# Up products of a bilinear layer: 15 products for three channel tiles and two token halves, with five additions of each triple on GpSimd

## The chip, the core and the metric

The kernel runs on one core of one Trainium2 chip. Its time is the device time of one execution in microseconds (us); the median of several runs is compared. TensorE is called PE in the profile (PEld for its weight loads), VectorE is DVE, ScalarE is ACT, GpSimd is POOL, and SyncE, which issues nearly all transfers here, is SP.

## What is computed

A linear attention with a decaying state (4 batches, 8 heads, 768 tokens, 48 channels a head), followed by a bilinear layer on the 3072 tokens with their 384 channels (1536 inner channels). All is fp32.

```python
for t in range(S):
    state = f[:, :, t, :, None] * state + np.einsum('bhd,bhe->bhde', k[:, :, t], v[:, :, t])
    y[:, :, t] = np.einsum('bhd,bhde->bhe', q[:, :, t], state)
...
a = x @ w_a
b = x @ w_b
return (a * b @ w_out).astype(np.float32)
```

## The kernel before

The 3072 tokens are eight blocks of 384 (BLK), two to a batch. For each block the attention has two units of four heads; their result lands transposed in xT (channels on the partitions: 3 tiles of 128 by 384 tokens). The up products a and b of a block are 12 inner tiles of 128 channels (NFT) by 384 tokens each, contracted over 3 channel tiles. Their elementwise product goes to a part of `groups`, and down products bring it back to 384 channels.

*Blocks 1 and 2* (the first batch) are made by up (L463): for one inner tile, 3 matmuls of 384 tokens for b and 3 for a, into two of the four PSUM banks ps_f; product (L478) copies b to SBUF on ScalarE (L484) and multiplies on VectorE (L486).

*Blocks 3 to 8* are made by up_pair (L528), two inner tiles (j) at a time, for both a and b (g). Of the three channel tiles, the first two are handled as a 2x2x2 block product (two inner tiles, two channel tiles, two token halves of 192) with 7 products for 8; the third takes 4. That is 11 calls of times (L540), each of two matmuls (b and a) of 192 tokens (L542). The products are accumulated in the four banks in such an order that intermediate sums are copied out once by ScalarE (L550, L553, L555, L559) and added to by VectorE (four additions L547 of a PSUM bank and an SBUF tile, called at L560 to L568); the two multiplications a*b per pair are L572. up_pair yields twice a pair, 12 times a block. The operands other than plain tiles are sums: of w, made once by combine_w_ba (L500; 8 VectorE instructions of 768 elements, L514) into the four `raw` buffers that the weight conversion has left; and of x, made for each block by combine_x (L520; four VectorE instructions of 192 elements, L526).

*Down* (L593) takes two groups of 128 tokens and makes 7 products for 8 in the same manner (L610), of 6 matmuls each. VectorE forms the sums s3, s1, s2, s4 in three rotating tiles `h` of 768 elements (L605 through the helper add), ScalarE copies u2, u3 and c11, VectorE adds, and SP stores the result tile o (L645, L649). Its first sum s3 is issued ahead of the last up products of the block; x1 needs s2, which needs the second half of the block's products.

*Attention*, for one unit u: front (L254) computes two sigmoids on ScalarE (L262 with an accumulator read, L264), one instruction on GpSimd (L266, 768 elements), two scans (L271), six scans (L281) and the products with q and k (L283, L284) on VectorE; then scores (matmuls L319, masked by L335), turn (transposes L347, copy to kT L351), gains (L367, sums L383), within (L401), across (L422, three copies y L435 and transfers to xT L450). front for the next unit is spread over the yields of slot (L652).

*Order of the work.* The program is written out by hand; each engine executes its instructions in the order in which they are called. The list `rest` holds the up and down work, and a counter `step` grows by one for each up, by one for each yield of up_pair and by 0.5 for each part of down. After each of these, beside (L844) continues the generators in `queue` that are due at that step: the slots of the attention, and combine_w_ba at 15.6, 16.6, 17.6 and 18.6 (L840). The plain up of blocks 1 and 2 ends with step 23, up of block 3 begins after 34.5. combine_x for the next block is called in the fifth part of the down ahead of it (L883). In the first 125 us the weights, which arrive as doubles, are converted: four ScalarE instructions, one on GpSimd (L205, 1.2 to 2.8 us) and two on VectorE (L214, L216); at the end combine_w_out (L580) makes the sums for down (L588 to L591).

The second kernel, by_levels, stands behind a condition on the data that doesn't hold here; the trace has none of its instructions.

Of the kernel before, what the change touches and what calls it, by code (L numbers as in the profile page):

```python
# [21 lines left out]
BLK = 384  # L22
# [11 lines left out]

# [3 lines left out]
def kernel(  # L44
# [30 lines left out]
    with tc.If(again > 0), ExitStack() as pools:  # L75
        by_levels(pools, tc, q, k, f_logit, v, masks, out, ident, weights)


def by_quotients(ctx, tc, q, k, f_logit, v, moe_w_a, moe_w_b, moe_w_out, out, ident, weights, bad):
# [27 lines left out]

# [18 lines left out]
    invs = [fixed([128, 2 * BLK], "inv"), spare[:, 3 * PIECE + PIECE // 2:3 * PIECE + PIECE // 2 + 2 * BLK]]  # L126
    tails = fixed([128, NU], "tails")
# [33 lines left out]
    def pieces():  # L161

        for ft, n in [(0, 1)] + [(ft, 2) for ft in range(1, NFT - 1, 2)] + [(NFT - 1, 1)]:
            for dst, src in ((w_b, moe_w_b), (w_a, moe_w_a)):
                cols = slice(ft * 128, (ft + n) * 128)
                yield dst[:, :, cols], src.rearrange("(kt p) c -> p kt c", p=128)[:, :, cols], (NKT, n * 128)
        for ft in range(0, NFT, 2):
            rows = moe_w_out[ft * 128:(ft + 2) * 128]
            yield w_out[:, ft:ft + 2], rows.rearrange("(k p) c -> p k c", p=128), (2, DM)

    EARLY = (4, 5)
    todo, raws, going = list(pieces()), [], []
# [18 lines left out]
    def from_double(dst, raw, k, bit):  # L191

        words = raw.bitcast(U32).rearrange("p k (n two) -> p (k n) two", two=2)
        lo, hi = words[:, :, 0], words[:, :, 1]
        width = lo.shape[1]
        h = sb3.tile([128, PIECE], FP32, tag="h", name="h")[:, 0:width]  # L200
        bit, sgn = bit[:, 0:width], sign[:, 0:width]
        nc.scalar.activation(h, hi.bitcast(FP32), AF.Abs, scale=HI_SCALE)  # L202

        nc.scalar.activation(bit.bitcast(FP32), lo, AF.Identity, bias=whole, scale=2.0**-29)
        nc.gpsimd.tensor_scalar(h, h, HI_MAX, None, ALU.min)  # L205
        yield
        nc.scalar.activation(sgn, hi.bitcast(FP32), AF.Sign)

        nc.scalar.activation(
            bit.bitcast(U16).rearrange("p (n two) -> p n two", two=2)[:, :, 1], sgn, AF.Relu, scale=-32768.0  # L210
        )
        yield
        hu = h.bitcast(U32)
        nc.vector.tensor_scalar(hu, hu, 3, None, ALU.logical_shift_left)  # L214
        hu, bit = (x.rearrange("p (k n) -> p k n", k=k) for x in (hu, bit))
        nc.vector.tensor_tensor(dst.bitcast(U32), hu, bit, ALU.add)  # L216
        yield

    def begin(n):

        while 2 * n > begun[0] < 2 * len(todo):
            i, second = divmod(begun[0], 2)
            dst, src, shape = todo[i]
            if not second:
                going.append(from_double(dst, raws[i], shape[0], bits[i % len(bits)]) if src.dtype != FP32 else iter(()))
            next(going[i], None)
            begun[0] += 1
# [65 lines left out]
    turns = itertools.cycle((0, 1))  # L293
# [184 lines left out]
    def product():  # L478
# [4 lines left out]
        b_sb = sb2.tile([128, BLK], FP32, tag="b_sb", name="b_sb")  # L483
# [6 lines left out]


    HT = BLK // 2
    sums_of_w, sums_of_x = [], {}

    def by_pairs(k):

        w = w_ba[:, :, k].rearrange("p g (j two c) -> p g two j c", two=2, c=128)
        return w[:, :, 0], w[:, :, 1]

    def combine_w_ba():  # L500

        (a11, a21), (a12, a22) = by_pairs(0), by_pairs(1)
        for _ in range(4):
            raw = raw_pool.tile([128, PIECE], mybir.dt.uint64, tag="raw", name="raw")
            sums_of_w.append(raw.bitcast(FP32).rearrange("p (g j c) -> p g j c", g=2, c=128))
        s1, s2, s3, s4 = sums_of_w
        for to, x, y, op in (
            (s3, a11, a21, ALU.subtract),
            (s1, a21, a22, ALU.add),
            (s2, s1, a11, ALU.subtract),  # L510
            (s4, a12, s2, ALU.subtract),
        ):
            for g in range(2):
                nc.vector.tensor_tensor(to[:, g], x[:, g], y[:, g], op)  # L514
            yield

    def blocks_of_x(blk, k):
        return (xT[blk][:, k, HT * i:HT * i + HT] for i in range(2))

    def combine_x(blk):  # L520

        (b11, b12), (b21, b22) = blocks_of_x(blk, 0), blocks_of_x(blk, 1)
        tiles = (sb2.tile([128, BLK], FP32, tag="b_sb", name="b_sb") for _ in range(2))
        t1, t2, t3, t4 = sums_of_x[blk] = [t[:, HT * i:HT * i + HT] for t in tiles for i in range(2)]
        for to, x, y in ((t1, b12, b11), (t2, b22, t1), (t3, b22, b12), (t4, b21, t2)):
            nc.vector.tensor_tensor(to, x, y, ALU.subtract)  # L526

    def up_pair(blk, j):  # L528

        (a11, a21), (a12, a22), (a1, a2) = (by_pairs(k) for k in range(NKT))  # L530
        (b11, b12), (b21, b22), (b1, b2) = (blocks_of_x(blk, k) for k in range(NKT))
        s1, s2, s3, s4 = sums_of_w
        t1, t2, t3, t4 = sums_of_x[blk]
# [717 lines left out]
```

## Time and profile before

| | |
|---|---|
| median of 3 runs | 626.2 us (626.1 to 627.07) |
| span of the profiled execution | 624.1 us; no other time of it is given, 2.1 us lie between it and the median |
| mean granted TensorE clock | 0.989 |
| plain up, blocks 1 and 2, to the end | until 145.5 us |
| down of the first batch | 145.5 to 202.4 us |
| up of blocks 3, 4, 5, 6, 7, 8 | 202.4, 267.2, 345.3, 409.8, 487.9 and 547.4 us to 249.6, 314.0, 392.2, 456.7, 533.0 and 590.4 us |
| last down | 590.4 to 624.1 us |
| up matmul records L542 | 1584, 296.6 us busy together |
| additions L547 on VectorE | 144, 557 ns each |
| multiplications L572 on VectorE | 72, 550 ns each |
| copies L550, L553, L555, L559 on ScalarE | 36 each, 479 ns |
| GpSimd after 125 us | L266 alone, 0.83 us each where nothing holds it |

A group's mean duration of a matmul (327 ns for 192 tokens) is longer than its share of PE's time, because matmuls overlap; the distance between the starts of groups says what one costs. In the order of time of one engine a line gives the start, the time until the end of the group, the engine, the line of the kernel, what is written and read, and in brackets the idle time ahead of it and what ended that.

### The profile page before, as it was taken

The numbers are of one execution on the slowest core, as the hardware profiler recorded it, in microseconds if no ns is written. First come the engines' busy times: TensorE is split into PE (matmuls) and PEld (weight loads), VectorE is DVE, ScalarE is ACT, GpSimd is POOL, SyncE is SP. The second block draws the span as 40 slices with busy tenths as digits, with TensorE's granted clock in tenths as the row PEclk, the third lists the DMA queues.
The fourth block names the chain that finished last, engine by engine and source line by source line (L and its number), as shares of the span: only waits on it lengthen the run. The fifth ranks groups of instructions, "written<-read, shape, count | busy, mean of one in ns | idle before, by whom it ended". The sixth has DMA issues, their size and how long they took to land.

```text
span 624.1 us, 13969 instructions
## 1 busy us (share of the span) xinstructions
PE 588.6 (94%) x5922; PEld 534.5 (86%) x5922; DVE 377.8 (61%) x748; ACT 221.6 (36%) x400; POOL 63.0 (10%) x58
## 2 busy tenths in 40 slices
PE   0759899999999999999999999999999999999995
PEld 0626555558998999999999999999999999999995
DVE  6777445797877567746676476756665244534541
ACT  5578499822332243224312332233311232022200
POOL 6334154410000000000000000000000000000000
PEclk9969999999999999999999999999999999999998
DMA  8886875000045404040404003050001000000000
GB/s 215 230 274 188 181 254 193 1 1 1 32 121 114 100 2 96 6 118 1 97 1 120 28 14 85 1 122 2 21 0 46 26 8 13 2 27 0 1 26 30
DMA packets 30343, 43.65 MB, mean 70 GB/s; under 512 B 3776, under 2 KB 24896, under 8 KB 30272
## 3 DMA queue, kind: packets, MB, share of 16 engines
q1 hardware_dynamic: 29984, 42.38, 25.2%
q8 instruction: 48, 0.79, 0.6%
q10 hardware_dynamic: 288, 0.30, 0.2%
q14 instruction: 23, 0.19, 0.1%
HBM read 33.23 MB, written 4.72 MB: 61 GB/s over the span
## 4 chain that ended last, share of the span: by engine, by line
PE 89%; DMA 4%; ACT 2%; DVE 2%; SPq 1%; issue 0%; ACTq 0%; DVEq 0%
PE ps_f L542 42%; PE ps_f L610 25%; PE ps_f L469 14%; DMA xT<-y 2%; PE ps_x L319 2%; PE ps_y L401 2%; PE ps_x L367 2%; PE ps_y L422 1%; PE ps_x L347 1%; DMA raw<-in_moe_w_b_dram 1%; DMA q_in<-in_q_dram 1%; SPq L154 1%; DVE h L605 0%; SPq L150 0%; ACTq L450 0%
## 5 line engine op out<-in xcount | busy, mean ns | idle before, releaser
L542 PE MATMUL ps_f<-xT,w_ba 128*128 128x192 f32 x864 | 155.7, 327 | 0.0
L547 DVE TENSOR_TENSOR groups<-ps_f,groups 128x384 f32<-128x384 f32 x144 | 80.1, 557 | 117.6 <-ACT groups L559 102.5
L542 PEld LDWEIGHTS ps_f<-xT,w_ba 128*128 128x128 f32 x864 | 142.3, 190 | 0.6
L469 PE MATMUL ps_f<-xT,w_ba 128*128 128x384 f32 x288 | 97.3, 497 | 7.5 <-DVE w_ba L216 6.0
L469 PEld LDWEIGHTS ps_f<-xT,w_ba 128*128 128x128 f32 x288 | 54.9, 193 | 47.1 <-DVE w_ba L216 7.1
L542 PE MATMUL ps_f<-b_sb,raw 128*128 128x192 f32 x432 | 82.2, 326 | 0.0
L542 PEld LDWEIGHTS ps_f<-b_sb,raw 128*128 128x128 f32 x432 | 72.2, 190 | 0.2 <-ACT groups L550 0.2
L610 PE MATMUL ps_f<-w_out,h 128*128 128x192 f32 x288 | 51.8, 330 | 0.0
L550 ACT COPY groups<-ps_f 128x384 f32<-128x384 f32 x36 | 17.2, 479 | 94.9 <-PE ps_f L542 94.8
L610 PE MATMUL ps_f<-w_out,groups 128*128 128x192 f32 x288 | 50.9, 327 | 0.0
L610 PE MATMUL ps_f<-spare,h 128*128 128x192 f32 x288 | 49.4, 327 | 0.2 <-DVE h L605 0.2
L610 PEld LDWEIGHTS ps_f<-w_out,groups 128*128 128x128 f32 x288 | 47.4, 190 | 0.1
L610 PEld LDWEIGHTS ps_f<-w_out,h 128*128 128x128 f32 x288 | 46.8, 190 | 0.6
L610 PEld LDWEIGHTS ps_f<-spare,h 128*128 128x128 f32 x288 | 46.8, 190 | 0.7 <-issue 0.5
L205 POOL TENSOR_SCALAR h<-h 128x768 f32<-128x768 f32 (+1 forms) x20 | 40.7, 2035 | 49.9 <-ACT h L202 49.9
L266 POOL TENSOR_SCALAR inv<-inv 128x768 f32<-128x768 f32 x14 | 13.5, 962 | 303.8 <-ACT inv L262 301.6
L572 DVE TENSOR_TENSOR groups<-groups 128x384 f32<-128x384 f32 x72 | 36.6, 550 | 0.0
L605 DVE TENSOR_TENSOR o<-ps_f,u 128x192 f32<-128x192 f32 x36 | 12.9, 357 | 39.1 <-PE ps_f L610 38.9
L559 ACT COPY groups<-ps_f 128x384 f32<-128x384 f32 x36 | 17.2, 479 | 53.0 <-PE ps_f L542 53.0
L435 ACT COPY y<-ps_y 48x384 f32<-48x384 f32 (+1 forms) x43 | 20.5, 476 | 25.9 <-PE ps_y L422 21.5
L542 PE MATMUL ps_f<-xT,raw 128*128 128x192 f32 x144 | 29.4, 327 | 0.0
L542 PE MATMUL ps_f<-b_sb,w_ba 128*128 128x192 f32 x144 | 29.3, 326 | 0.0
(113 smaller groups left out, 691.3 us busy)
## 6 DMA issues: line engine op xcount, KB each, us to landing
q_in<-in_q_dram SPq DMA_DIRECT2D x32, 144.0 KB, 4.5
k_in<-in_k_dram SPq DMA_DIRECT2D x32, 144.0 KB, 3.6
v_in<-in_v_dram SPq DMA_DIRECT2D x16, 288.0 KB, 5.1
raw<-in_moe_w_out_dram SPq DMA_DIRECT2D x6, 768.0 KB, 4.4
out_dram<-o SPq DMA_DIRECT2D x24, 192.0 KB, 1.9
f_in<-in_f_logit_dram SPq DMA_DIRECT2D x28, 144.0 KB, 3.0
xT<-y SPq DMA_DIRECT2D x46, 72.0 KB, 2.2
raw<-in_moe_w_b_dram SPq DMA_DIRECT2D x4, 768.0 KB, 7.3
```

The source lines that it names most:

```text
L205: nc.gpsimd.tensor_scalar(h, h, HI_MAX, None, ALU.min)
L266: nc.gpsimd.tensor_scalar(inv, inv, EXP_K, 1.0, ALU.mult, ALU.add)
L319: nc.tensor.matmul(ps[h][SUB * p:SUB * p + SUB, o:o + SUB], lhsT=kf[r, tokens(n, c, p)], rhs=qf[r, tokens(n, c, p)], start=True, stop=True,)
L435: copy(y[r:r + rows, :, p], ps[p][e:e + rows, 0:BLK].rearrange("r (o m) -> r o m", m=SUB))
L469: nc.tensor.matmul(ps[nm][:, 0:BLK], lhsT=w[:, kt, ft * 128:ft * 128 + 128], rhs=x[:, kt], start=kt == 0, stop=kt == NKT - 1,)
L542: nc.tensor.matmul(to[:, g], lhsT=w[:, g, j], rhs=x, start=start and g == 0, stop=True, skip_group_check=True)
L547: nc.vector.tensor_tensor(c[:, :, k, i], x, y, ALU.add)
L550: nc.scalar.copy(p1, x0)
L559: nc.scalar.copy(u3, x0)
L572: nc.vector.tensor_tensor(to[:, :, 2 * j + k], a[:, :, k], b[:, :, k], ALU.mult)
L605: nc.vector.tensor_tensor(to, x, y, op)
L610: nc.tensor.matmul(to, lhsT=x[:, i], rhs=w[:, i], start=first and i == 0, stop=i == HFT - 1, skip_group_check=True)
```

## The change

Up products of blocks 3 to 8 are made by up_triples in place of up_pair: three inner tiles (j of 4) at a time, all three channel tiles, two token halves, with 15 products for 18, named v1 to v6, u1 to u5, t1, t2, r2, r3 after the bank in which they are summed. In each bank the next product is added to the last after an intermediate state was copied out. Of the results, six are written by a ScalarE copy (`first`, and the one in `finish`), four additions read PSUM on VectorE (`add`), and for five more ScalarE copies the bank to a temporary and GpSimd adds the temporary to the result (`late`). `finish` (v6, its copy and one VectorE multiplication of 1152 elements) of a triple is called behind the first product of the next one, and for the last triple of a block at once. up_triples yields three times a triple, 12 times a block as before.

combine_w_ba makes six sums and two tiles of w_ba in place, in 26 GpSimd instructions of 512 elements, at steps 15.6 to 22.8 (nine times two) and from 24.2 on (four times two). combine_x makes its sums in 11 VectorE instructions, some in place in xT. The tiles h and b_sb lie at fixed places in `sums` and `x_sums`, as many as before (three and two); u3 of down lies in o. In by_levels, which isn't executed, the weights are converted anew.

```diff
@@ -124,6 +174,13 @@
     bits = [spare[:, PIECE * i:PIECE * i + PIECE].bitcast(U32) for i in range(3)]
     sign = spare[:, 3 * PIECE:3 * PIECE + PIECE // 2].bitcast(BF16)
     invs = [fixed([128, 2 * BLK], "inv"), spare[:, 3 * PIECE + PIECE // 2:3 * PIECE + PIECE // 2 + 2 * BLK]]
+
+    sums = fixed([128, 3 * PIECE], "sums")
+    thirds = [sums[:, PIECE * i:PIECE * i + PIECE] for i in range(3)]
+    blocks = itertools.cycle(thirds)
+    last = groups[:, NTG + 1:2 * NTG].rearrange("p g c -> p (g c)")
+    x_sums = fixed([128, 5 * (BLK // 2)], "x_sums")
+    b_copies = itertools.cycle([x_sums[:, BLK * i:BLK * i + BLK] for i in range(2)])
     tails = fixed([128, NU], "tails")
     held = fixed([128, NU, 2], "held")
 
...
@@ -480,102 +501,168 @@
         if not factors:
             return
         blk, ft, ps = factors.pop(0)
-        b_sb = sb2.tile([128, BLK], FP32, tag="b_sb", name="b_sb")
+        b_sb = next(b_copies)
         nc.scalar.copy(b_sb, ps["b"][:, 0:BLK])
         a, b = (x.rearrange("p (g t) -> p g t", g=NTG) for x in (ps["a"][:, 0:BLK], b_sb))
         nc.vector.tensor_tensor(products(blk)[:, :, ft], a, b, ALU.mult)
         give_back(ps.values())
 
 
-
-
     HT = BLK // 2
-    sums_of_w, sums_of_x = [], {}
-
-    def by_pairs(k):
-
-        w = w_ba[:, :, k].rearrange("p g (j two c) -> p g two j c", two=2, c=128)
-        return w[:, :, 0], w[:, :, 1]
...
     def combine_w_ba():
 
...
+        halves = []
         for _ in range(4):
...
+            raw = raw_pool.tile([128, PIECE], mybir.dt.uint64, tag="raw", name="raw").bitcast(FP32)
+            halves += [raw[:, 512 * i:512 * i + 512].rearrange("p (j c) -> p j c", c=128) for i in range(3)]
+        s = [halves[2 * i:2 * i + 2] for i in range(6)]
+        (a11, a12, a13), (a21, a22, a23), (a31, a32, a33) = (
+            [[w_ba[:, g, k].rearrange("p (j i c) -> p i j c", i=NI, c=128)[:, i] for g in range(2)] for k in range(NKT)]
+            for i in range(NI)
+        )
         for to, x, y, op in (
...
+            (s[0], a21, a32, ALU.add),
+            (s[1], a12, a22, ALU.add),
+            (s[2], s[1], a21, ALU.add),
+            (s[1], s[1], a23, ALU.add),
+            (s[3], a12, s[1], ALU.subtract),
+            (s[3], s[3], a32, ALU.subtract),
+            (s[4], a31, a11, ALU.subtract),
+            (s[5], s[4], a32, ALU.add),
+            (s[4], a33, s[4], ALU.subtract),
+            (a22, s[1], s[4], ALU.subtract),
+            (a22, a22, a13, ALU.add),
+            (a31, a31, a33, ALU.subtract),
+            (a31, a31, a21, ALU.add),
         ):
             for g in range(2):
...
+                nc.gpsimd.tensor_tensor(to[g], x[g], y[g], op)
             yield
...
+        sums_of_w.update(
+            v1=s[0], v2=a32, v3=s[3], v4=s[1], v5=a12, v6=s[2],
+            u1=a21, u2=a31, u3=s[4], u4=a11, u5=s[5],
+            t1=a22, t2=a13, r2=a23, r3=a33,
+        )
 
     def combine_x(blk):
 
...
+        x = xT[blk].rearrange("p k (i t) -> p k i t", i=2)
+        (b11, b12), (b21, b22), (b31, b32) = ([x[:, k, i] for i in range(2)] for k in range(NKT))
+        s = x_sums.rearrange("p (n t) -> p n t", t=HT)
+        more = last[:, 2 * NI * BLK:].rearrange("p (n t) -> p n t", t=HT)
+        u5, u3, v6, v1, u1 = (s[:, n] for n in range(5))
+        v2, v4, t2, r2 = (more[:, n] for n in range(4))
+
+        def op(to, x, y, op):
+            nc.vector.tensor_tensor(to, x, y, op)
+
+        op(s[:, 0:2], x[:, 0], b31.unsqueeze(1).broadcast_to((128, 2, HT)), ALU.add)
+        op(v1, b21, u5, ALU.subtract)
+        op(v6, b31, b21, ALU.subtract)
+        op(b11, b11, b12, ALU.subtract)
+        op(u1, b11, v6, ALU.add)
+        op(r2, b22, b32, ALU.subtract)
+        op(v2, b22, v1, ALU.subtract)
+        op(v4, b22, b31, ALU.subtract)
+        op(t2, b32, b31, ALU.subtract)
+        op(b32, b12, b32, ALU.add)
+        op(b21, b21, b22, ALU.subtract)
+        sums_of_x[blk] = dict(
+            v1=v1, v2=v2, v3=b22, v4=v4, v5=b21, v6=v6,
+            u1=u1, u2=b12, u3=u3, u4=b11, u5=u5,
+            t1=b31, t2=t2, r2=r2, r3=b32,
+        )
+
+    def up_triples(blk):
+
+        to, tail = products(blk), None
+
+        def times(ps, name, j, start=False):
             for g in range(2):
                 nc.tensor.matmul(
...
+                    ps[:, g],
+                    lhsT=sums_of_w[name][g][:, j],
+                    rhs=sums_of_x[blk][name],
+                    start=start and g == 0,
+                    stop=True,
+                    skip_group_check=True,
                 )
 
...
+        def finish(j, c, out, v):
+            times(v, "v6", j)
+            nc.scalar.copy(out[1, 0], v)
+            a, b = (
+                c[:, g].rearrange("p k i t -> p k (i t)").rearrange("p k (g t) -> p g k t", g=NTG) for g in range(2)
+            )
+            nc.vector.tensor_tensor(to[:, :, NI * j:NI * j + NI], a, b, ALU.mult)
+
+        for j in range(NJ3):
+            v, u, r, t = (ps_f[i][:, 0:BLK].rearrange("p (g t) -> p g t", g=2) for i in free)
+            free[:] = [free[i] for i in (2, 3, 1, 0)]
+            c = (sums, last[:, 0:2 * NI * BLK])[j % 2].rearrange("p (g k i t) -> p g k i t", g=2, k=NI, i=2)
+            out = {(k, i): c[:, :, k, i] for k in range(NI) for i in range(2)}
+            if j % 2:
+                at = (thirds.index(down_first[0]) + 1) * 2
+                places = [(at + n) % 6 for n in range(4)]
+                spaces = sums
+            else:
+                places, spaces = range(4), last
+            temps = [spaces[:, BLK * n:BLK * n + BLK].rearrange("p (g t) -> p g t", g=2) for n in places]
+
+            def first(k, i, ps):
+                nc.scalar.copy(out[k, i], ps)
+
+            def late(k, i, ps, temp):
+                nc.scalar.copy(temp, ps)
+                nc.gpsimd.tensor_tensor(out[k, i], out[k, i], temp, ALU.add)
+
+            def add(k, i, ps):
+                nc.vector.tensor_tensor(out[k, i], ps, out[k, i], ALU.add)
+
+            times(v, "v1", j, True)
+            first(2, 0, v)
+            if tail:
+                finish(*tail)
+            times(u, "u1", j, True)
+            first(1, 1, u)
+            times(r, "r2", j, True)
+            add(1, 1, r)
+            times(v, "v2", j)
+            first(2, 1, v)
+            times(u, "u2", j)
+            late(2, 1, u, out[1, 0])
+            yield
+            times(t, "t1", j, True)
+            first(0, 0, t)
+            times(v, "v3", j)
+            late(1, 1, v, temps[0])
+            times(u, "u3", j)
+            first(0, 1, u)
+            times(r, "r3", j, True)
+            add(2, 1, r)
+            times(v, "v4", j)
+            late(0, 1, v, temps[1])
+            yield
+            times(u, "u4", j)
+            late(0, 0, u, temps[2])
+            times(t, "t2", j)
+            add(0, 1, t)
+            times(v, "v5", j)
+            late(0, 0, v, temps[3])
+            times(u, "u5", j)
+            add(2, 0, u)
+            tail = j, c, out, v
+            if j == NJ3 - 1:
+                finish(*tail)
+            yield
 
     HM = DM // 2
     combos = []
+    down_first = [thirds[0]]
 
     def combine_w_out():
 
...
@@ -599,7 +686,8 @@
         a21, a22 = (products(blk1)[:, g1, HFT * i:HFT * i + HFT] for i in range(2))
 
         def block():
-            return sb3.tile([128, PIECE], FP32, tag="h", name="h").rearrange("p (k t) -> p k t", k=HFT)
+            down_first[0] = thirds[(thirds.index(down_first[0]) + 1) % 3]
+            return thirds[thirds.index(down_first[0]) - 1].rearrange("p (k t) -> p k t", k=HFT)
 
         def add(to, x, y, op=ALU.add):
             nc.vector.tensor_tensor(to, x, y, op)
@@ -613,7 +701,10 @@
 
         s3 = add(block(), a21, a11, ALU.subtract)
         yield
-        x, m = ps_f[0:2] if next(turns) else ps_f[2:4]
+        if not free:
+            free.extend(idle)
+        x, m = (ps_f[i] for i in free[0:2])
+        free[:] = free[2:4] + free[1::-1]
         x0, x1, m0, m1 = (t[:, HM * i:HM * i + HM] for t in (x, m) for i in range(2))
         times(x0, a11, b11, True)
         u2 = sb2.tile([128, HM], FP32, tag="u2", name="u2")
@@ -623,7 +714,9 @@
         s2 = add(block(), s1, a11, ALU.subtract)
         yield
         times(m1, s3, t3, True)
-        u3 = sb1.tile([128, HM], FP32, tag="u3", name="u3")
+        o = sb1.tile([128, 2, DM], FP32, tag="o", name="o")
+        c11, c12, c21, c22 = (o[:, i, HM * j:HM * j + HM] for i in range(2) for j in range(2))
+        u3 = c21
         nc.scalar.copy(u3, m1)
         s4 = add(block(), a12, s2, ALU.subtract)
         yield
@@ -634,8 +727,6 @@
         add(u3, u2, u3)
         yield
         times(x0, a12, b21)
-        o = sb1.tile([128, 2, DM], FP32, tag="o", name="o")
-        c11, c12, c21, c22 = (o[:, i, HM * j:HM * j + HM] for i in range(2) for j in range(2))
         add(c22, m0, u3)
         yield
         times(m0, s4, b22)
...
@@ -809,8 +899,8 @@
         for b in range(B):
             even, odd = ([(blk, g) for g in range(NTG)] for blk in (2 * b, 2 * b + 1))
             if b:
-                rest += [(up_pair, 2 * b, j) for j in range(NFT // 2)] + [(down, b, tuple(even[1:]))]
-                rest += [(up_pair, 2 * b + 1, j) for j in range(NFT // 2)]
+                rest += [(up_triples, 2 * b, j) for j in range(NFT)] + [(down, b, tuple(even[1:]))]
+                rest += [(up_triples, 2 * b + 1, j) for j in range(NFT)]
             else:
                 rest += [(down, b, tuple(even[1:]))]
             rest += [(down, b, (even[0], odd[0])), (down, b, tuple(odd[1:]))]
@@ -836,8 +926,8 @@
             queue += [((m - 1) * a_batch + d, slots[s]) for d in when] if s > 4 * NQ else [
                 (d, slots[s]) for d in begun_early[s - 2 * NQ]
             ]
-        sums = combine_w_ba()
-        queue += [(d, sums) for d in (15.6, 16.6, 17.6, 18.6)]
+        for_w = combine_w_ba()
+        queue += [(15.6 + 0.9 * n, for_w) for n in range(9)] + [(24.2 + 0.9 * n, for_w) for n in range(5)]
         queue.sort(reverse=True, key=lambda x: x[0])
         step, ahead = 5, None
 
@@ -861,12 +951,14 @@
                     next(ahead)
                 step += 1
                 continue
-            if what is up_pair:
-                for _ in up_pair(blk, i):
-                    step += 1
-                    beside()
-                if i == 2 + blk % 2:
-                    ahead = down(rest[n + NFT // 2 - i][2])
+            if what is up_triples:
+                if i == 0:
+                    this = up_triples(blk)
+                next(this)
+                step += 1
+                beside()
+                if i == NFT - NI:
+                    ahead = down(rest[n + NI][2])
                     next(ahead)
                 continue
             if (blk, i) == (B - 1, tuple(even[1:])):
```

## The prediction

> **What bounds the kernel now.** I read the first part of the page (busy shares), then the chain that ended last, then the table by stage, and only then the order of time of single engines where the change works.
>
> ```profile
> PE 588.6 (94%) x5922; PEld 534.5 (86%) x5922; DVE 377.8 (61%) x748; ACT 221.6 (36%) x400; POOL 63.0 (10%) x58
> ...
> PE 89%; DMA 4%; ACT 2%; DVE 2%; SPq 1%; issue 0%; ACTq 0%; DVEq 0%
> ```
>
> TensorE is 89% of the chain. The table by stage (stretch, length, then busy time of PE, PEld, DVE, ACT, POOL, then clock, DMA) shows how complete that is: in the first up stage of the old kind (202.4 to 249.6) PE is busy 47.13 of 47.20 us.
>
> ```profile
> 145.50:202.40 56.90, 56.01 (x917) 53.50 (x917) 45.57 (x99) 15.87 (x31) 2.49 (x3) 1.00 0.30 73
> 202.40:249.60 47.20, 47.13 (x465) 46.44 (x464) 31.04 (x65) 17.27 (x34) 1.66 (x2) 1.00 0.29 67
> ```
>
> So a product taken from PE there is worth its full time, unless a wait comes in its place. The price of a product is in PE's order of time: 8 records (two products of two matmuls, each matmul two records) start 1.30 us before the next group, so 0.65 us a product.
>
> ```profile
> 203.72 1.46 PE L542 MATMUL ps_f<-b_sb,raw 128*128 128x192 f32 x8
> 205.02 0.81 PE L542 MATMUL ps_f<-b_sb,w_ba 128*128 128x192 f32 x4
> ```
>
> **What the skill says.** (1) The Trainium skill, "GPSIMD Engine Reference", section 3.1: an add of two fp32 tensors of 2048 elements takes 4497 ns on GpSimd. No run here has such an add. As an estimate from that page, in proportion: 0.84 us for 384 elements, 1.12 us for 512. (2) "SBUF — State Buffer", section "Who interferes with whom": a VectorE instruction with two SBUF inputs and a GpSimd instruction that reads SBUF exclude each other; one with a PSUM input does not. The trace agrees. GpSimd's L266, usually 0.83 us, took 1.95 while VectorE combined weights, and the next combination took 1.98 where its three likes take 1.35: one waited for the other, in turn, and VectorE lost 0.63.
>
> ```profile
> 129.60 1.36 DVE L590 TENSOR_TENSOR spare<-w_out,spare 128x1152 f32<-128x1152 f32 x1
> 130.88 1.98 DVE L591 TENSOR_TENSOR w_out<-w_out 128x1152 f32<-128x1152 f32 x1
> ...
> 129.71 1.95 POOL L266 TENSOR_SCALAR inv<-inv 128x768 f32<-128x768 f32 x1 [9.22 <-ACT inv L262]
> ```
>
> Beside the additions L547, which read PSUM, L266 costs neither side anything (248.7 us: 0.83, and L547 0.56). (3) "TensorE: Matmul & The Clock Gate", the section on the array's detail: ScalarE and VectorE work strictly in order. The trace shows nothing else, and the ScalarE step below rests on it.
>
> **Part 1, the products (removed).** A block now has 6 pairs of 11 products, 66; after, 4 triples of 15, 60 (the built order has 720 up matmuls for 792). Six blocks: 36 products x 0.65 = **-23.4 us**, all on the path.
>
> **Part 2, copies on ScalarE (added).** Copies per block rise from 24 to 44 (six results taken first or last by ScalarE, five more copied out for GpSimd, times four). At 0.48 us (L550) that is 5.3 of the 9.75 us of a triple: no bound by its sum. What matters is the distance. A bank's next product waits for the copy of its last one. The trace: product at 202.42, its copy L550 at 203.27, for 0.48; the copy ends 1.33 after the product began. In the new order a copied bank's next product comes three products later, at 1.95: 0.62 to spare, as now between a11 and s2, where PE does not wait. So the ordinary copy costs nothing. Not so when ScalarE does something else between: the two sigmoids of front.
>
> ```profile
> 221.52 0.48 ACT L559 COPY groups<-ps_f 128x384 f32<-128x384 f32 x1 [1.47 <-PE ps_f L542]
> 221.90 0.94 ACT L262 ACTIVATE inv<-f_in,less 128x768 f32<-128x768 f32 x1
> 222.74 0.19 ACT L262 ACTIVATION_READ_ACCUMULATOR inv<-f_in,less 128x1 f32 x1
> 222.96 0.84 ACT L264 ACTIVATE f_in<-f_in 128x768 f32<-128x768 f32 x1
> 226.47 0.48 ACT L550 COPY groups<-ps_f 128x384 f32<-128x384 f32 x1 [2.67 <-PE ps_f L542]
> ```
>
> They hold ScalarE 1.8 us after the copy (222.0 to 223.8). Today they fall into a gap of 2.7 us. In the built order of after, six pairs fall into up stages: five directly behind the copy of v4, ahead of that of u4, one at a triple's end. With a triple's start as zero: v4 begins at 6.50, its copy ends 7.83, sigmoids until 9.63, copy of u4 until 10.05; u5, due at 9.10, needs it, a semaphore and a weight load of 0.19: 10.3. Wait 1.2 x 5, and 0.3 for the sixth, whose next copy isn't needed before two more products: **+6.3**. Bounds: 3 (half hidden by other waits of PE) and 9.
>
> **Part 3, the end of a block (added).** In the last triple v6 follows v5 by two products, 1.30, for a copy that takes 1.33 plus the weight load: 0.3 x 6. Then the multiplication of three tiles (1.35, from L588) must follow, where two of 0.55 stood, before the two sums of down. Today PE already waits once 0.2 for these (537.31, below); I add 0.2 in the four blocks with no attention matmuls as cover: together **+2.5**, bounds 1 and 5.
>
> ```profile
> 535.22 0.95 DVE L605 TENSOR_TENSOR h<-groups 128x768 f32<-128x768 f32 x1
> 536.21 0.96 DVE L605 TENSOR_TENSOR h<-h,groups 128x768 f32<-128x768 f32 x1
> ...
> 537.31 4.14 PE L610 MATMUL ps_f<-spare,h 128*128 128x192 f32 x24 [0.21 <-DVE h L605]
> ```
>
> **Part 4, sums of x (added).** combine_x grows from 4 operations (191.87 to 193.10, 1.23 us) to 11, one of them double width: 11 x 0.31 pitch + 0.2 = 3.6. At five of six places VectorE idles 1.8 to 2.4 us right behind it or nothing urgent follows: nothing (were that cover gone, up to 2.4 each). The first is in the chain: q and k of a front are queued behind it and the scores wait for them.
>
> ```profile
> 193.10 0.95 DVE L283 TENSOR_TENSOR q_in<-q_in,f_in 128x768 f32<-128x768 f32 x1
> 193.97 0.95 DVE L284 TENSOR_TENSOR k_in<-k_in,inv 128x768 f32<-128x768 f32 x1
> ...
> 194.97 1.03 PE L319 MATMUL ps_x<-q_in,k_in 48*64 48x64 f32 x48 [0.73 <-DVE k_in L284]
> ```
>
> PE waits already, so **+2.4**, bounds 1.5 and 3.
>
> **Part 5, sums of w (moved and grown).** Eight L514 (7.3 us) leave VectorE; 26 additions of 512 elements go to GpSimd, x 1.12 = 29 us, in GpSimd's queue ahead of three L266, from 116 us to about 165. GpSimd itself has time (two are needed only at 202). But VectorE works there without a gap from 119 to 143, mostly on two SBUF inputs. By the turn-taking above each collision costs it 0.63 x 1024/768 = 0.8 (1024 elements read for 768). About 12 collide between 127 and 150: 9.6, less 1.8 for the L514 at 132.8, less the 2.8 between k's end (142.7) and the scores (145.5): about 4 of waiting. The last eight start once the plain up matmuls have let go of w_ba; four meet the scans and sums ahead of s2, where there is no slack at all.
>
> ```profile
> 150.76 0.96 DVE L605 TENSOR_TENSOR h<-h,groups 128x768 f32<-128x768 f32 x1
> ...
> 151.82 4.17 PE L610 MATMUL ps_f<-spare,h 128*128 128x192 f32 x24
> ```
>
> 4 x 0.8 = 3.2. Together **+7**; bounds 0 (they fall beside PSUM work) and 15 (all 20 at 0.93, less the cover).
>
> **Part 6, at no cost.** Five additions a triple on GpSimd: 5 x 0.84 = 4.2 of 9.75, their results due one triple's head later; the copy that overwrites a temporary has over 2 us. VectorE's own work per block falls (36 x 0.555 = 20 to 16 x 0.557 + 4 x 1.35 = 14.3). u3 now lies in o, so its copy waits for the store before: issue at 162.34, landing 1.9, against a copy at 168 (were the store late, ScalarE's queue would stand behind it). SP's queue keeps its order; no load moves. by_levels isn't run. If GpSimd's addition took over 2 us, the triple would hang on it: rival below.
>
> **Sum.** -23.4 + 6.3 + 2.5 + 2.4 + 7 = -5.2. On the profiled span: 624.1 - 5.2 = 618.9; the page gives only its span, and the median of the runs, 626.2, stands 2.1 above: **621.0**.
>
> **Rivals.** *A, the covers hold*: GpSimd's sums find VectorE at PSUM work or idle (part 5: 0), sigmoids 3, ends 1.5, x 2.4. For it: 61% VectorE; against: 119 to 143 without a gap. 626.2 - 16.5 = 609.7. *B, slower*: one mechanism, GpSimd's sums of w keep VectorE from SBUF between 116 and 170 us. All 20 collide at 0.93 (18.6), cover 3.6: 15 of PE's waiting, so 626.2 - 23.4 + 15 + 11.2 = 629.0. It decides from 12.2 us of waiting in that stretch. For it: PE there has 0.8 to 2.8 us of slack; against: GpSimd's queue leaves gaps when L266 waits for ScalarE. *C, ScalarE becomes the pace of a triple*: 0.62 to spare less 0.19 is thin; if copies or GpSimd's additions run late by 1 us a triple, 24 us: 645. Against: the same distance holds today. That fewer products aren't made is excluded by the built order.
>
> **Chances.** Forecast 0.47 (616 to 626: faster 0.41, same 0.03, slower 0.03), A 0.28 (faster), B 0.20 (slower 0.17, same 0.03), C 0.05 (slower). Faster 0.69, same 0.06, slower 0.25; 0.2% is about what a measurement of this kernel tells from no change. The range 609 to 630 leaves out C, the upper half of B and the lower part of A, some 0.2.
>
> **What would show it.** PE waiting for ScalarE's copy some 1.2 us at each of five sigmoid pairs, and nowhere else in a triple; scores near 195 waiting 3 us for k; waits of PE for VectorE between 130 and 165 of 7 us, with VectorE's two-input rows lengthened beside GpSimd's additions; these about 1.1 us (512) and 0.84 (384) long. Wrong if an up triple takes over 9.8 us without sigmoids, or if VectorE's rows keep their length beside GpSimd.

## Result: 1.4% slower, where 0.8% faster was forecast

The kernel after the change takes 635.6 us (median of 4 runs, 634.9 to 636.5), the kernel before 626.6 us on the same chip (4 runs, 626.1 to 627.4): ratio 1.0137, 95% interval 1.0122 to 1.0153. The forecast was 621.0, the range 609 to 630. Line numbers of "after" are those of the changed kernel.

The profiled execution of after has a span of 634.4 us (before: 624.1). First the busy shares.

```profile
PE 578.7 (91%) x5778; PEld 517.9 (82%) x5778; DVE 389.7 (61%) x686; ACT 277.4 (44%) x520; POOL 230.5 (36%) x204
```

PE is busy 9.9 us less than before (588.6 us), and the kernel is 10 us longer: what grew is PE's waiting. The order of time of PE tells where (the starts of the stages, in us):

| stage | before | after | change |
|---|---|---|---|
| until the first triple (before: pair) of block 3 starts | 202.4 | 221.5 | +19.1 |
| up stages of blocks 3 to 8, lengths | 47.2, 46.8, 46.9, 46.8, 45.1, 43.0 | 47.9, 45.5, 45.7, 45.5, 41.2, 39.3 | -10.7 |
| all down stages from block 3 on | | | +1.9 |

The two up stages without a front beside them (41.2, 39.3) are 3.9 and 3.7 us shorter, as 6 products of 0.65 should make them. The four others are not, and block 3's is longer than before. The list of waits (engine, line waited for and its engine and line: us in all, times, longest) names who ends PE's waiting. In after, L586 is an up product, L698 a down product and L340 the scores; L306 is the product with k, L624 VectorE's addition out of PSUM (`add`), L620 ScalarE's copy for a late result, L693 a sum of down:

```profile
PE ps_x L340 <- DVE k_in L306: 8.9, 2, 5.9
PE ps_f L586 <- DVE sums L624: 5.2, 5, 1.1
PE ps_f L698 <- DVE sums L693: 4.2, 5, 2.7
...
PE ps_f L586 <- ACT sums L620: 3.9, 5, 0.8
```

Before, the first and third of these were 0.7 and 0.2 us and the others didn't exist. The two waits of the first line (5.9 and 3.0 us) and the longest of the third lie ahead of block 3. PE's order of time shows two of them, after and then at the same place before:

```profile
154.25 1.56 PE L340 MATMUL ps_x<-q_in,k_in 48*64 48x64 f32 x48 [5.88 <-DVE k_in L306]
155.74 3.63 PE L698 MATMUL ps_f<-w_out,groups 128*128 128x192 f32 x12
...
165.38 5.85 PE L698 MATMUL ps_f<-spare,sums 128*128 128x192 f32 x24 [2.72 <-DVE sums L693]
```

```profile
145.53 0.93 PE L319 MATMUL ps_x<-q_in,k_in 48*64 48x64 f32 x48
146.38 2.22 PE L610 MATMUL ps_f<-w_out,groups 128*128 128x192 f32 x12
```

Two losses are to be read here, not one. PE waits 5.88 and 2.72 us for VectorE. And behind each wait the same work takes longer than in before: the scores 1.56 for 0.93, the next 12 records 3.63 for 2.22, the 24 records 5.85 for 4.17. The table by stretch (length, busy time of PE, PEld, DVE, ACT, POOL, then the granted clock, the DMA's share and its GB/s) shows what goes with it, at the places behind the three long waits:

```profile
155.70:159.20 3.50, 3.50 (x17) 3.45 (x13) 3.32 (x3) 0.86 (x2) 3.42 (x3) 0.58 0.02 5
165.35:171.05 5.70, 5.67 (x24) 5.67 (x25) 4.80 (x11) 0.00 (x0) 4.27 (x3) 0.70 0.00 0
213.50:217.10 3.60, 3.60 (x14) 3.57 (x13) 2.83 (x4) 1.08 (x3) 0.83 (x1) 0.56 0.02 5
```

The clock is 0.56 to 0.70 there and 1.00 in the neighbouring stretches. VectorE's order of time shows why it was late, beside GpSimd's; the last two lines are the same scans in before:

```profile
144.78 1.02 DVE L303 TENSOR_TENSOR_SCAN inv<-inv,zero 128x128 f32<-128x128 f32 x1
145.72 2.76 DVE L303 TENSOR_TENSOR_SCAN inv<-inv,start,zero 128x128 f32<-128x128 f32 x2
148.40 1.41 DVE L303 TENSOR_TENSOR_SCAN inv<-inv,zero 128x128 f32<-128x128 f32 x1
...
146.82 2.71 POOL L543 TENSOR_TENSOR raw<-raw,w_ba 128x512 f32<-128x512 f32 x2
149.49 2.71 POOL L543 TENSOR_TENSOR raw<-w_ba,raw 128x512 f32<-128x512 f32 x2
```

```profile
138.78 0.40 DVE L281 TENSOR_TENSOR_SCAN inv<-inv,zero 128x128 f32<-128x128 f32 x1
139.09 0.83 DVE L281 TENSOR_TENSOR_SCAN inv<-inv,start,zero 128x128 f32<-128x128 f32 x2
```

These scans took 0.40 (one) and 0.83 (two) in before. Here, from the second on, each takes as long as one addition on GpSimd, 1.36 us (2.71 for two): the engines go in step, one instruction of each in turn. That is what the prediction called a collision. It expected twelve between 127 and 150 us, of instructions "mostly on two SBUF inputs", without saying which. Here the scans, the comparison L294 (0.16 before, 1.05 now) and the conversion's L64 (0.55 before, 1.54 now) collide as well: between 121 and 153 us seventeen instructions of VectorE take 13.5 us longer than in before, and 8.0 of that falls on the scans and the comparison. The additions that read PSUM (L507, 0.55) keep their length.

### The profile page after: what moved, and what is told of

It reads as the page before. It is cut to its first block, busy times and chain, and to the rows that moved or that the text cites. A ratio compares the mean times of both kernels' runs of the same rounds, so it can differ in the third digit from the quotient of the medians.

```text
span 634.4 us, 14052 instructions
## 1 busy us (share of the span) xinstructions
PE 578.7 (91%) x5778; PEld 517.9 (82%) x5778; DVE 389.7 (61%) x686; ACT 277.4 (44%) x520; POOL 230.5 (36%) x204
## 5 line engine op out<-in xcount | busy, mean ns | idle before, releaser
L586 PE MATMUL ps_f<-xT,w_ba 128*128 128x192 f32 x480 | 95.2, 327 | 0.0
L490 PEld LDWEIGHTS ps_f<-xT,w_ba 128*128 128x128 f32 x288 | 55.2, 195 | 48.2 <-issue 6.3
L586 PEld LDWEIGHTS ps_f<-xT,w_ba 128*128 128x128 f32 x480 | 80.3, 190 | 0.4
L586 PE MATMUL ps_f<-x_sums,raw 128*128 128x192 f32 x384 | 73.9, 330 | 3.9 <-ACT sums L620 3.9
L586 PEld LDWEIGHTS ps_f<-x_sums,raw 128*128 128x128 f32 x384 | 63.3, 190 | 6.6 <-ACT sums L620 6.3
L624 DVE TENSOR_TENSOR sums<-ps_f,sums 128x384 f32<-128x384 f32 x48 | 26.0, 551 | 54.3 <-PE ps_f L586 47.5
L621 POOL TENSOR_TENSOR sums<-sums,groups 128x384 f32<-128x384 f32 x48 | 48.9, 1028 | 22.8 <-ACT groups L620 18.9
L621 POOL TENSOR_TENSOR groups<-groups,sums 128x384 f32<-128x384 f32 x48 | 50.2, 1050 | 16.5 <-ACT sums L620 15.1
L698 PE MATMUL ps_f<-spare,sums 128*128 128x192 f32 x288 | 51.3, 335 | 4.2 <-DVE sums L693 4.2
L586 PE MATMUL ps_f<-groups,w_ba 128*128 128x192 f32 x288 | 54.9, 326 | 0.0
L698 PE MATMUL ps_f<-w_out,sums 128*128 128x192 f32 x288 | 53.3, 336 | 0.0
L624 DVE TENSOR_TENSOR groups<-ps_f,groups 128x384 f32<-128x384 f32 x48 | 26.6, 555 | 42.8 <-PE ps_f L586 26.9
L698 PEld LDWEIGHTS ps_f<-spare,sums 128*128 128x128 f32 x288 | 48.4, 196 | 5.4 <-DVE sums L693 2.8
L698 PE MATMUL ps_f<-w_out,groups 128*128 128x192 f32 x288 | 52.3, 333 | 0.0
L698 PEld LDWEIGHTS ps_f<-w_out,groups 128*128 128x128 f32 x288 | 48.8, 195 | 0.2
L698 PEld LDWEIGHTS ps_f<-w_out,sums 128*128 128x128 f32 x288 | 48.3, 195 | 0.7
L586 PEld LDWEIGHTS ps_f<-groups,w_ba 128*128 128x128 f32 x288 | 48.1, 190 | 0.3 <-ACT groups L617 0.3
```

The costliest lines, as they stand in the source:

```text
L490: nc.tensor.matmul(ps[nm][:, 0:BLK], lhsT=w[:, kt, ft * 128:ft * 128 + 128], rhs=x[:, kt], start=kt == 0, stop=kt == NKT - 1,)
L586: nc.tensor.matmul(ps[:, g], lhsT=sums_of_w[name][g][:, j], rhs=sums_of_x[blk][name], start=start and g == 0, stop=True, skip_group_check= ...
L621: nc.gpsimd.tensor_tensor(out[k, i], out[k, i], temp, ALU.add)
L624: nc.vector.tensor_tensor(out[k, i], ps, out[k, i], ALU.add)
L698: nc.tensor.matmul(to, lhsT=x[:, i], rhs=w[:, i], start=first and i == 0, stop=i == HFT - 1, skip_group_check=True)
```

## Experiments

All are changes of the kernel after unless said otherwise, and ratios are against the kernel before on the same chip. The experiments ran on three chips, on which the kernel before took 626.8 to 627.2 us (626.6 beside after), so differences in us from after are good to about half a us. The theory after reading the trace: (1) GpSimd's 26 additions of w hold VectorE up ahead of block 3, and PE's clock falls behind the waits; (2) in the triples, the scans of a front stand in VectorE's queue ahead of the additions of t2 and u5, and the sigmoids in ScalarE's queue ahead of the copy of u4. Rivals: VectorE is simply too full; the path over ScalarE and GpSimd is too long for a triple.

**The additions of w left out.** In combine_w_ba the loop goes, and plain parts of w_ba stand for the sums:

```diff
...
-            for g in range(2):
-                nc.gpsimd.tensor_tensor(to[g], x[g], y[g], op)
-            yield
+        s = [a11, a12, a21, a31, a11, a12]
...
```

> The changed kernel without the 26 additions of w on GpSimd: the products take parts of w_ba in their place, so the up results are not the reference's; everything else is as in the changed kernel. Theory (GpSimd's additions hold VectorE up between 116 and 170 us): the scores that waited 5.9 us and the sums that waited 2.7 us no longer wait, the slow-clock stretches behind them (about 3.5 us) go too, the first triple starts near 209 us instead of 221.5, and the time is about 623. Rival (VectorE's own queue is too full there, with or without GpSimd): first triple at 218 or later, time 632 or more.

Measured: 622.4 us, ratio 0.9921 (0.9892 to 0.995): 13.2 us less than with them. The first triple starts at 207.8. PE's order of time at the place of the 5.88 us wait:

```profile
147.08 0.93 PE L340 MATMUL ps_x<-q_in,k_in 48*64 48x64 f32 x48
147.94 2.22 PE L682 MATMUL ps_f<-w_out,groups 128*128 128x192 f32 x12
```

Wait and slow matmuls are both gone. Leaving the additions out wins about 13 us, where the forecast put their cost at 7.

**The same additions on VectorE.**

```diff
-                nc.gpsimd.tensor_tensor(to[g], x[g], y[g], op)
+                nc.vector.tensor_tensor(to[g], x[g], y[g], op)
```

> The same 26 additions at the same places, on VectorE. Theory (what costs is the two engines taking turns, about 0.95 us for each VectorE instruction): VectorE's own work grows by 26 x 0.62 = 16 us, less than the 17 us of lengthened rows that go, and the first of it falls into idle gaps of 1.85 us; scores wait 2 to 5 us, time 627 to 633. Rival (the stretch is bound by VectorE's sum of work): 16 us more in a full queue, time 640 or more.

Measured: 626.6 us, ratio 1.0001 (0.9988 to 1.0015), a little better than the theory's range. VectorE is busy 16.1 us more than with the additions left out (386.1 for 370.0), but 3.6 less than in after (389.7), and the kernel is 9 us faster than after. One addition takes VectorE 0.68 us, a pair 1.28; on GpSimd it takes 1.3 alone, and lengthens the instruction of VectorE that meets it by about 0.95. Between 147 and 163 us PE's waits left are 0.24, 0.97, 0.72 and 1.42 us, and the matmuls behind the longest keep their 2.22 us.

**The additions in halves, on GpSimd.**

```diff
-                nc.gpsimd.tensor_tensor(to[g], x[g], y[g], op)
+                for j in (slice(0, 2), slice(2, 4)):
+                    nc.gpsimd.tensor_tensor(to[g][:, j], x[g][:, j], y[g][:, j], op)
```

> Each of the 26 additions on GpSimd in two of half the columns (256 elements), 52 in all. Theory (each VectorE instruction with SBUF inputs waits for one GpSimd instruction to end): a collision costs VectorE half, about 0.5 us instead of 0.95, there are more of them, spread further; the scores wait 2 to 4 us less, time 630 to 634. Rival (the loss goes with the amount of data read): VectorE loses the same, time 635 to 637.

Measured: 630.3 us, ratio 1.0056 (1.0036 to 1.0075), 5.3 us less than after. The scores wait 2.85 instead of 5.88 us, and the wait of 2.72 falls to 0.18; a new one of 1.27 comes at the next scores. VectorE and GpSimd side by side:

```profile
141.59 1.68 DVE L303 TENSOR_TENSOR_SCAN inv<-inv,start,zero 128x128 f32<-128x128 f32 x2
143.19 0.88 DVE L303 TENSOR_TENSOR_SCAN inv<-inv,zero 128x128 f32<-128x128 f32 x1
...
141.29 3.29 POOL L544 TENSOR_TENSOR raw<-raw,w_ba 128x256 f32<-128x256 f32 x4
```

A scan now takes 0.8, as one half addition does (3.29 for four). So the price of a collision goes with GpSimd's instruction and not with what VectorE reads: beside whole additions a scan of 128 elements (0.40 to 1.36) and a sum of 1152 (L676, 1.36 to 2.31) both lose about 0.95 us, beside halves both lose 0.4 (the same sum then takes 1.77). The loss is 0.3 to 0.4 us less than GpSimd's instruction takes alone (1.30 and 0.72).

**The kernel before with its eight sums of w on GpSimd** (one part of the change alone; 768 elements each).

```diff
-                nc.vector.tensor_tensor(to[:, g], x[:, g], y[:, g], op)
+                nc.gpsimd.tensor_tensor(to[:, g], x[:, g], y[:, g], op)
```

> The kernel before, with only its eight sums of w (768 elements) moved from VectorE to GpSimd: one part of the change alone. Theory (turn-taking): VectorE is rid of 7.3 us and loses about 1.5 us in each of eight collisions, 12 in all; 2.8 us of slack ahead of the scores, so 0 to 4 us slower than before: 626 to 630. Rival (GpSimd's work is free beside VectorE): same or up to 1 us faster, 625 to 626.

Measured: 631.7 us, ratio 1.007 (1.0043 to 1.0098). The direction is the theory's, the size was taken too small. The wait came at another place, where the plain up products wait for the multiplication L486 to free their banks, and the slow clock with it.

```profile
140.31 11.64 PE L469 MATMUL ps_f<-xT,w_ba 128*128 128x384 f32 x30 [3.44 <-DVE groups L486]
```

In after, the same 30 records behind a wait of 0.41 us take 9.94. VectorE's sums of 1152 elements (L589, L590) take 2.85 us beside additions of 768, for 1.36 before: 1.5 a collision, as the theory had it. Taking 7.3 us of work from VectorE makes the kernel 5 us slower.

**Scans moved to the end of a triple** (five places; the times at which front's third step is due):

```diff
-            (33.4, 33.4, 33.9, 33.9, 36.1, 38.1),
-            (39.1, 40.1, 41.1, 41.1, 42.1, 44.1),
+            (33.4, 33.4, 33.9, 33.9, 37.1, 38.1),
+            (39.1, 40.1, 41.1, 41.1, 43.1, 44.1),
...
-                (2.6, 3.6, 4.6, 5.6, 7.6, 9.6),
-                (10.6, 12.3, 13.3, 14.3, 17.1, 19.1),
+                (2.6, 3.6, 4.6, 5.6, 8.6, 9.6),
+                (10.6, 12.3, 13.3, 14.3, 18.1, 19.1),
```

> The changed kernel with the six scans of a front (the second step of its VectorE work) moved, at the five places where they fall behind the product v4 of a triple, to the end of that triple. Theory (the scans, lengthened by GpSimd's additions, stand ahead of the additions of t2 and u5 in VectorE's queue, and the next triple's u1 waits for the bank that t2's addition frees): five waits of about 1.05 us, 1.2 with what follows, go; time about 629.5. Rival (the additions wait for GpSimd's sums, not for the scans): the waits stay, time 635 to 636.

Measured: 629.7 us, ratio 1.0049 (1.0032 to 1.0066), 5.9 us less than after. The line L586 <- L624 is gone from the waits; the one for the copy of u4 grew, to the 1.2 us of the prediction:

```profile
PE ps_f L586 <- ACT sums L620: 6.2, 5, 1.2
```

That the time meets the theory's 629.5 so well is in part luck. In the trace the up stages are only 4.3 us shorter than in after (260.9 for 265.2). Another 1.6 us is a slow stretch that is missing: the scores at 212 us wait 3 us as in after, but the matmuls behind them keep their 2.22 us (3.75 in after).

```profile
212.01 1.03 PE L340 MATMUL ps_x<-q_in,k_in 48*64 48x64 f32 x48 [3.02 <-DVE k_in L306]
212.97 2.22 PE L698 MATMUL ps_f<-w_out,sums 128*128 128x192 f32 x12
```

**Sigmoids moved too** (the edit against the run before). At two of the five places the sigmoids alone move; at the other three the attention's scores and the two steps behind them move by one as well.

```diff
-            (39.1, 40.1, 41.1, 41.1, 43.1, 44.1),
+            (40.1, 41.1, 42.1, 42.1, 43.1, 44.1),
...
-                (10.6, 12.3, 13.3, 14.3, 18.1, 19.1),
-                (20.1, 21.1, 22.1, 23.1, 25.1, 27.8),
+                (11.6, 12.3, 13.3, 14.3, 18.1, 19.1),
+                (21.1, 22.1, 23.1, 24.1, 25.1, 27.8),
```

> As the run with the scans moved, and the five sigmoid pairs that fall behind v4 are moved to the end of the triple too. Theory: five waits of 0.8 us for the copy of u4 (0.9 with what follows) go as well, another 4.5 us: about 625. Rival (at the end of a triple the sigmoids hold up v6 and the next triple's copies just as long): no gain over the run before, 629.5.

Measured: 623.2 us, ratio 0.9941 (0.9925 to 0.9958), another 6.5 us less. No wait of L586 for anything is left, also where the sigmoids alone moved, and PE fills the up stages (table by stretch, blocks 3 and 4):

```profile
221.80:265.20 43.40, 43.33 (x440) 42.43 (x439) 30.05 (x50) 24.30 (x50) 21.48 (x20) 1.00 0.30 73
282.80:326.00 43.20, 43.20 (x425) 42.39 (x424) 27.56 (x46) 24.21 (x50) 21.25 (x21) 1.00 0.31 74
```

All six stages sum to 253.4 us, for 275.8 before: 22.4 less. So the path over ScalarE and GpSimd is not too long; only its order against the fronts was.

**The five late results added by VectorE**, straight from PSUM:

```diff
-                nc.scalar.copy(temp, ps)
-                nc.gpsimd.tensor_tensor(out[k, i], out[k, i], temp, ALU.add)
+                nc.vector.tensor_tensor(out[k, i], ps, out[k, i], ALU.add)
```

> The changed kernel with the five late results of a triple added by VectorE straight from PSUM, without ScalarE's copy and GpSimd's addition. VectorE then has nine additions of 0.56 and a product of 1.36 in a triple, 6.4 of 9.75 us. Theory (GpSimd's additions cost through the scans alone): scans fall back from 4.4 to 2.6 us and the sigmoid waits go (4.5 us), but the addition of u4 now stands behind the scans and u5 waits 1.5 to 2 us at five places; sum about nothing: 631 to 637. Rival (the path over ScalarE and GpSimd is what makes triples slow): all waits in triples go, 624 to 627.

Measured: 643.9 us, ratio 1.0282 (1.0262 to 1.0301), 8 us slower than after and outside both ranges: the rival is out, and the theory named the wait but missed how many there would be (14 of 1.1 us on average, not five). The scans are short again (438.83 to 440.96), but four additions stand behind them, each of which holds a bank:

```profile
439.30 0.81 PE L586 MATMUL ps_f<-xT,w_ba 128*128 128x192 f32 x4
441.55 1.24 PE L586 MATMUL ps_f<-x_sums,raw 128*128 128x192 f32 x6 [1.43 <-DVE sums L620]
```

**The sums of x half a step later**, behind q and k of the front:

```diff
-                if part == 4 and rest[n + 1:] and rest[n + 1][0] is up_triples:
+                if part == 5 and rest[n + 1:] and rest[n + 1][0] is up_triples:
```

> The changed kernel with the 11 sums of x issued half a step later, behind the q and k of the front at the first place. Theory: the wait of 3.0 us of the scores at 212 falls to about 0.5, the slow stretch behind it (1.5 us) goes, nothing else waits for the sums: about 631.5. Rival (the first triple then waits for the sums of x, or other blocks do): 635 or more.

Measured: 630.0 us, ratio 1.0049 (1.0032 to 1.0066), 5.6 us less than after. The wait of 3.03 us before the scores is gone altogether, and no triple waits for the sums. The wait of 2.72 us is 2.15 in this execution, and the matmuls behind it are slow all the same (4.17 us at full clock):

```profile
166.08 5.85 PE L698 MATMUL ps_f<-spare,sums 128*128 128x192 f32 x24 [2.15 <-DVE sums L693]
```

**GpSimd's late additions left out** (the copies stay):

```diff
-                nc.gpsimd.tensor_tensor(out[k, i], out[k, i], temp, ALU.add)
```

> The changed kernel without the five additions of a triple on GpSimd (the copies to the temporaries stay, so the up results are not the reference's); scans and sigmoids stay behind v4. Theory (the scans are long because GpSimd's additions hold them up): the scans fall back from 4.4 to 2.6 us, the additions of t2 and u5 come in time and the five waits of 1.05 us for VectorE go; the five waits for the copy of u4 grow from 0.8 to about 1.2, as in the run with the scans moved. Time 635.6 - 6 + 0 to 2 = 630 to 632. Rival (the scans are in the way whatever their length): waits for VectorE stay, 635 to 637.

Measured: 627.9 us, ratio 1.0012 (1.0005 to 1.0019). The waits for L624 are gone though the scans stay where they were: it is GpSimd that makes them too long. In the order of time of VectorE, first with, then without its additions:

```profile
434.70 1.60 DVE L303 TENSOR_TENSOR_SCAN inv<-inv,start,zero 128x128 f32<-128x128 f32 x2
436.22 1.15 DVE L303 TENSOR_TENSOR_SCAN inv<-inv,zero 128x128 f32<-128x128 f32 x1
437.30 1.53 DVE L303 TENSOR_TENSOR_SCAN inv<-inv,start,zero 128x128 f32<-128x128 f32 x2
438.75 0.99 DVE L624 TENSOR_TENSOR sums<-ps_f,sums 128x384 f32<-128x384 f32 x2
```

```profile
428.52 0.83 DVE L303 TENSOR_TENSOR_SCAN inv<-inv,start,zero 128x128 f32<-128x128 f32 x2
429.27 0.40 DVE L303 TENSOR_TENSOR_SCAN inv<-inv,zero 128x128 f32<-128x128 f32 x1
429.59 0.83 DVE L303 TENSOR_TENSOR_SCAN inv<-inv,start,zero 128x128 f32<-128x128 f32 x2
430.34 1.12 DVE L623 TENSOR_TENSOR sums<-ps_f,sums 128x384 f32<-128x384 f32 x2
```

The up stages are 6.9 us shorter than in after (258.3 for 265.2). The time is 2 us below the theory's, which fits the sigmoid waits: they stayed at 0.79 and did not grow to 1.2. In the run with the scans moved, the sigmoids began 0.34 us late behind k's multiplication, which GpSimd held up (1.75 us for 0.95); here nothing holds it.

**All three together.** Scans and sigmoids moved, sums of x later, the additions of w on VectorE; once at their old places, once where VectorE is idle (with the two in-place tiles in the other order):

```diff
-        queue += [(15.6 + 0.9 * n, for_w) for n in range(9)] + [(24.2 + 0.9 * n, for_w) for n in range(5)]
+        queue += [(n, for_w) for n in (16, 17, 18, 19, 20, 21, 22, 27, 28.9, 31.2, 32.2, 33.35, 34.4, 34.4)]
```

> The same three edits, but the additions of w on VectorE at the places they have in the changed kernel. Theory: 608.5, as the sum of the three single gains; 2 to 4 us behind the run with new places. Rival (the places don't matter): the same time as that run.

> The changed kernel with three edits together: scans and sigmoids at the end of a triple, sums of x half a step later, and the 26 additions of w on VectorE, at places where VectorE was idle (seven pairs between steps 16 and 22, six pairs one by one between steps 27 and 34.5). Theory (independent stretches, so the gains add): 635.6 - 12.5 - 5.6 - 9.0 for the additions at their old places = 608.5, and 3 us less where the new places avoid the waits of 0.2 to 1.4 us that the old ones left: 605 to 609. Rival (the additions move the waits to other places of VectorE's full queue): 611 or more.

Measured: old places 609.4 us, ratio 0.9716 (0.9702 to 0.9731); new places 606.8 us (5 runs), ratio 0.9672 (0.9659 to 0.9685). The gains add, and this version is 3.3% faster than the kernel before.

```profile
148.20:204.40 56.20, 55.22 (x877) 52.65 (x870) 52.16 (x111) 16.45 (x33) 3.74 (x4) 1.00 0.28 73
204.40:247.80 43.40, 43.33 (x439) 42.43 (x439) 32.55 (x59) 24.29 (x50) 21.48 (x20) 1.00 0.32 73
```

The first down stretch takes 56.2 us again (56.9 in before), with VectorE busy 93% of it.

## Why the prediction was wrong, step by step

Numbers are of the profiled executions. A wait in the triples costs 0.26 us more than itself: the ten waits are 9.1 us, and the six up stages are 265.1 us with them and 253.4 without, 11.7.

| step of the prediction | forecast | measured | from |
|---|---|---|---|
| 1, products | -23.4 | -22.4 | 275.8 us of up stages before, 253.4 with scans and sigmoids moved |
| 2, sigmoids | +6.3 | +5.2 | five waits, 3.9 + 5 x 0.26 |
| 3, ends of blocks | +2.5 | +1.9 | down stages |
| 4, first sums of x | +2.4 | +3.9 | wait 3.0 for 0.7, and 1.6 of slow clock |
| 5, sums of w | +7 | +12.7 | waits 0.4 + 5.9 + 2.7, and 3.7 of slow clock |
| 6, the rest | 0 | +6.5 | five waits for L624, 5.2 + 5 x 0.26 |
| sum | -5.2 | +7.8 | |

The spans differ by 10.3. Of the rest, 2.1 lies before 76 us, where the execution of after was later; other executions of like kernels reach that place between 72.7 and 75.8 us, so I don't count it to the change; 0.4 stays open.

*Steps 1 to 3 held*, 2 down to its five places. The 22.4 of step 1 is 23.5 less the wait of v6 at six block ends (0.19 us each), which the prediction had under step 3; step 3 is then +3.0. *Step 4* sized the wait rightly (2.3 more) and left out that PE runs slowly afterwards.

*Step 5* is the first term that was mis-sized: +7 forecast, +12.7 measured. Its own sum has a slip (9.6 less 1.8 less 2.8 is 5.0, not "about 4"), which would have made it 8.2. "About 12 collide between 127 and 150 ... 4 of waiting" became 6.3, with more collisions (the seventeen lengthened instructions, 13.5 us, for twelve and 9.6); "four meet the scans and sums ahead of s2 ... 3.2" was 2.7. The waits, 9.0 for 7.2, are near the forecast; the 3.7 us of slow clock were not in it. Rival B named this mechanism, and 12.2 us of waiting as the point from which it decides: the waits alone didn't reach it, with the slow clock the loss did. B's own time, 629.0, still took the rest of the sum for granted.

*Step 6* failed outright: a term put at nothing that measured +6.5 (6.9 by the up stages of the run without the late additions). "Part 6, at no cost. Five additions a triple on GpSimd" looked at GpSimd's own time and at VectorE's total, which falls; it did not ask what GpSimd's additions do to the scans, though step 5 had the rule for it. And it did not place the scans against the triple as step 2 placed the sigmoids. The run with the scans moved and the one without the late additions each take these waits away.

Rival C is out: the undisturbed stages need 9.8 us a triple (39.3 for four). Rival A's premise, covers that hold, is what the last version arranges.

## To carry to other kernels

Work moved from VectorE to GpSimd is not free beside it: each of GpSimd's SBUF instructions can delay one of VectorE's by nearly its own length, so near a deadline of VectorE it costs more than doing the work there (0.95 us against 0.65 an addition here). When a schedule of buffers becomes tighter, place every long burst of every in-order queue against it, not only that of one engine. And a wait of TensorE from about 2 us on may cost another 1.7 us here, for the slow clock behind it.

## What the runs showed of the hardware

- Between 60 and 600 us these traces have 22 waits of PE of 2.15 to 5.89 us. With 21 of them, during the wait or within 2 us of its end, the granted clock fell to 0.50, mostly for about 3.4 us, which costs 1.7 us of work (1.6 to 3.1 over all). With the one of 3.02 us shown under the moved scans it stayed at 1.00, as with every wait up to 1.75 us, and nowhere else in these stretches did it fall. The Trainium skill, "TensorE: Matmul & The Clock Gate", section "What's actually happening", has the clock halved after an idle window of about 3.4 us that runs freely. The half clock and the 3.4 us agree; but 2.15 us of waiting were enough here and 3.02 once were not, so a wait shorter than that figure is not safe, and a single run doesn't tell what a wait will cost. That the wait is the cause is inferred from their going together: in each run that removed a wait, the slow stretch behind it went. Why one wait had none stays open.
- The same skill, "SBUF — State Buffer", section "Who interferes with whom", calls the ports that VectorE and GpSimd share an exclusive lock. The runs agree that the two take turns, and show the steady state: one instruction of each engine in turn, 1.36 us a scan beside additions of 512 elements and 0.8 beside those of 256. But 0.3 to 0.4 us of the two instructions overlap (1.36 for a scan of 0.40 and an addition of 1.30).
- GpSimd's fp32 addition took 1.00 us for 384 elements, 1.30 for 512 and 1.85 for 768 where it ran alone; the estimates in proportion, 0.84 and 1.12, were 14 to 16% low. Beside VectorE the additions of 512 took up to 2.4 us.
